# Attention, dense FFN and routed experts on one core: a scratch row 96 bytes longer, the last logits in five per two chunks, two weight splits a chunk earlier

## The chip, the cores and the metric

One core of a Trainium2 chip runs the whole program. Times are device microseconds of one execution; the result of a kernel is the median of several executions. TensorE is PE in the profile (its weight loads PEld), VectorE DVE, ScalarE ACT, GpSimd POOL, and SP issues most of the DMAs.

## The reference, cut to what matters

```python
x = attention(q, k, v)                      # 4 x 8 heads, 576 positions, rotary; -> 2304 tokens x 512
x = square(relu(x @ w_in)) @ w_out          # 512 -> 2048 -> 512
logits = x @ w_gate + modality_bias[modality_id]        # 8 experts
e_idx = argmax(logits, axis=1); gate_w = softmax(logits)[e_idx]
for e in range(8):
    mask = e_idx == e
    out[mask] = gate_w[mask, None] * (relu(x[mask] @ w1[e]) @ w2[e])    # 512 -> 1024 -> 512
```

All of it is float32.

## The kernel before, in words

Attention goes first, by a list of steps written out by hand, and reaches into the start of the dense layer. Then comes `experts`, which this change touches. It works in units, each a pair of matmul groups on TensorE, with two units of lookahead: in unit q the first half of unit q + 2 is issued and then the second half of unit q.

**The dense layer** has 80 units: five blocks of tokens (four of 512, the last of 256) by 16 chunks of 128 hidden features. The first half is `mm1` (12 matmuls: 4 pieces of the contraction by three passes over high and low parts, stationary operand from the weights, moving operand from the tokens `xs`). ScalarE makes `r` and its square `gh`, the low part `gl` comes from VectorE (`rest`, L680), and in the last block ScalarE squares once more into the PSUM tile `h` (L674). The second half is `mm2` (three matmuls for each 128 tokens, stationary `gh` or `gl`, moving the weights, 512 columns).

**The expert layer** has the same shape in units of 128 hidden features of one expert: `emm1` (L984, stationary `w`, moving the gathered tokens `ye` or `yee`), then `emm2` (L1007, stationary `ge`, `geh`, `gel` or `gl`, moving `w`). Each chunk of expert weights is loaded (`eissue`) and split into two parts by ScalarE and VectorE (`esplit`, L937 and L938). Before the first expert its tokens are gathered and transposed (`gtrans`, L957, L970, L971).

**The logits** of a 128-token tile are eight reductions on VectorE (`lg_dve`, L710), whose full-size output `junk` goes to PSUM. Those of the fourth block (three tiles this way, 24 reductions) run in the chunks of the last block, which start at unit n0 = 64; the fourth tile goes over TensorE in the first two chunks (`lg_tr`, `lg_mm`).

**Two resources matter here.** The first is a ring of four PSUM buffers, which `bank` and the tiles `h` take in rotation: each `h`, `tp`, `lp`, `junk` takes the buffer that was taken four requests earlier, and waits until the last reader of that one is done. The second is where tiles lie in SBUF. The weights `wf` and `w`, and the `ye` and `yee` tiles that later take the place of `wf`, are in pools on the left. `we` (the weights of one chunk in sixteen, number 4), `xs`, `r`, and the ring of `gh`, `gl`, `ge`, `geh` and `gel` are in the pool `m_sb` on the right, which ends at the top of the memory. The tiles stand in it in the order of their first use, upwards.

The schedule is a table: `at(mid, n, f)` puts f between the two halves of unit n, `at(pre, n, f)` ahead of both.

Of the kernel before, what the change touches and what calls it, by code (L numbers as in the profile page):

```python
# [9 lines left out]
F32 = mybir.dt.float32  # L10
# [24 lines left out]
def f32(ap):  # L35
    return ap.bitcast(F32)
# [480 lines left out]
def experts(tc, wts, ps, xT, rD, wexp, mod, wg, mb, cst, ident, yD, out):  # L517
    nc = tc.nc
    with ExitStack() as ctx:
        sb = ctx.enter_context(tc.tile_pool(name="m_sb", bufs=1, side="right", reuse_waits="tile"))  # L520
# [12 lines left out]
        def bank(shape, name):  # L533
            return ps.tile(shape, F32, name=name, tag="b", bufs=4)
# [11 lines left out]
        def xraw(b, k):  # L546
            t0, n = BLOCKS[b]
            if b == 1:
                t = wts.pool.tile([128, n], F32, name="xraw", tag="wraw", bufs=NRAW)
                nc.sync.dma_start(out=t, in_=xT[k, :, 0, t0:t0 + n])  # L550
                raws[b, k] = t
                return
            x = t2([128, n], F32, "xraw")
            if k == 0:
                rbs[b] = sb.tile([128, n], F32, name="rbs", tag="xs", bufs=5)
            nc.sync.dma_start(out=x, in_=xT[k, :, 0, t0:t0 + n])
            raws[b, k] = x
            xrec(b, k, rbs[b])
# [16 lines left out]
        def xnorm(b, k, eng):  # L575
            x = raws[b, k]
            eng.tensor_tensor(out=x, in0=x, in1=rbs.pop((b, k)), op=ALU.mult)  # L577

        def xhigh(b, k):
            x = raws[b, k]  # L580
            n, o = BLOCKS[b][1], OFF * (BLOCKS[b][1] <= SLOT)
            t = sb.tile([128, 2 * n + o], F32R, name="xs", tag="xs", bufs=5)
            t = xs[b, k] = t[:, o:o + 2 * n].rearrange("p (a n) -> p a n", a=2)
            nc.scalar.activation(out=t[:, 0], in_=x, func=ACTF.Copy)

        def xlow(b, k):
            t = xs[b, k]
            nc.vector.tensor_tensor(out=t[:, 1], in0=raws.pop((b, k)), in1=f32(t[:, 0]), op=ALU.subtract)
# [119 lines left out]
        def lg_dve(j, e):  # L708
            junk = bank([128, DM], "junk")
            nc.vector.scalar_tensor_tensor(out=junk, in0=ysb[j], scalar=1.0, in1=wgb[e], op0=ALU.mult, op1=ALU.mult,  # L710
                                           accum_out=lg[:, j, e:e + 1])
# [20 lines left out]

        def choose(j0, j1):
            js, shp = slice(j0, j1), [128, j1 - j0, E]
            mx = sb.tile([128, 4], F32, name="mx", tag="mx", bufs=1)[:, 0:j1 - j0]
            km = sb.tile([128, 4], F32, name="km", tag="km", bufs=1)[:, 0:j1 - j0]
            k = sb.tile([128, 4, E], F32, name="ky", tag="ky", bufs=1)[:, 0:j1 - j0]
            d = sb.tile([128, 4, E], F32, name="dl", tag="dl", bufs=1)[:, 0:j1 - j0]
            nc.vector.tensor_tensor(out=lg[:, js], in0=lg[:, js], in1=bias[:, js], op=ALU.add)
            nc.vector.tensor_reduce(out=mx, in_=lg[:, js], axis=AX.X, op=ALU.max)  # L740
            mxb = mx.unsqueeze(2).to_broadcast(shp)
            nc.vector.tensor_tensor(out=k, in0=lg[:, js], in1=mxb, op=ALU.is_ge)
            nc.vector.scalar_tensor_tensor(out=k, in0=k, scalar=-16.0, in1=c_io8.unsqueeze(1).to_broadcast(shp),
                                           op0=ALU.mult, op1=ALU.add)
            nc.vector.tensor_tensor(out=d, in0=lg[:, js], in1=mxb, op=ALU.subtract)
            nc.vector.tensor_reduce(out=km, in_=k, axis=AX.X, op=ALU.min)
            nc.vector.tensor_tensor(out=oh[:, js], in0=k, in1=km.unsqueeze(2).to_broadcast(shp), op=ALU.is_equal)
            nc.vector.tensor_copy(out=ohb[:, js], in_=oh[:, js])
            for j in range(j0, j1):
                nc.vector.tensor_tensor(out=cum[:, j + 1], in0=cum[:, j], in1=ohb[:, j], op=ALU.add)  # L750
            nc.scalar.activation(out=d, in_=d, func=ACTF.Exp)
            nc.vector.tensor_reduce(out=gate[:, js], in_=d, axis=AX.X, op=ALU.add)
            nc.vector.tensor_scalar(out=gate[:, js], in0=gate[:, js], scalar1=1e-9, scalar2=None, op0=ALU.add)
            nc.vector.reciprocal(out=gate[:, js], in_=gate[:, js])

        def ranks(j0, j1):
            js = slice(j0, j1)
            rp = bank([128, j1 - j0, E], "rp")
            nc.tensor.matmul(out=rp, lhsT=lt_b, rhs=ohb[:, js], start=True, stop=False)
            nc.tensor.matmul(out=rp, lhsT=one_b, rhs=cum[:, js], start=False, stop=True)  # L760
            nc.vector.tensor_copy(out=rank[:, js], in_=rp)

        def counts(j):
            cp = bank([128, E], "cp")
            nc.tensor.matmul(out=cp, lhsT=one_b, rhs=cum[:, j], start=True, stop=True)
            tables["n"] = cp
# [158 lines left out]
        def eissue(m):  # L925
            s, f = divmod(m, EFC)
            if f == 0:
                src = es0[0:1, 0:1] if s == NE - 1 else esi[0:1, s:s + 1]
                regs[s] = nc.sync.value_load(src, min_val=0, max_val=E - 1)
            r = wts.pool.tile([128, 1024], F32, name="eraw", tag="wraw", bufs=NRAW)  # L930
            nc.sync.dma_start(out=r, in_=wexp[bass.ds(regs[s], 1), f].rearrange("o p n -> p (o n)"))
            eraw[m] = r

        def esplit(m, nxt=None):
            w = wts.ring.tile([128, 2, 1024], F32R, name="w", tag="w", bufs=NFC - NF0 - NF1)
            r = eraw.pop(m)
            nc.scalar.activation(out=w[:, 0], in_=r, func=ACTF.Copy)  # L937
            nc.vector.tensor_tensor(out=w[:, 1], in0=r, in1=f32(w[:, 0]), op=ALU.subtract)  # L938
            ew[m] = w
            if nxt is not None:  # L940
                eissue(nxt)
# [76 lines left out]
        M0, M1 = (NE - 1) * EFC, (LAST + 1) * EFC  # L1018
        N = NB * NFC
        pre, mid, post = {}, {}, {}  # L1020

        def at(d, n, *fs):
            d.setdefault(n, []).extend(fs)

        at(mid, NFC - 1, load_wgb)
        for b in range(NB):
            if b:
                q = NFC * b
                for k in range(4):
                    if b > 1:  # L1030
                        at(mid, q - 11 + 2 * k, lambda b=b, k=k: xraw(b, k))
                        at(mid, q - 10 + 2 * k, lambda b=b, k=k: xnorm(b, k, nc.gpsimd))
                        at(mid, q - 3, lambda b=b, k=k: [xhigh(b, k), xlow(b, k)])
            j0, nt = BLOCKS[b][0] // 128, BLOCKS[b][1] // 128
            n0 = NFC * (b + 1)
            if b < 3:
                jobs = [(j, e) for j in range(j0, j0 + nt) for e in range(E)]
                for q, (j, e) in enumerate(jobs):
                    at(mid, n0 + q // 3, lambda j=j, e=e: lg_dve(j, e))
                at(mid, n0 + 11, lambda j0=j0, nt=nt: choose(j0, j0 + nt))  # L1040
                if b < 2:
                    at(mid, n0 + 13, lambda j0=j0, nt=nt: ranks(j0, j0 + nt))
                    continue
                at(post, n0 + 13, lambda j0=j0, nt=nt: ranks(j0, j0 + nt), lambda: counts(NT0), early1)
                at(post, n0 + 15, early2)
                at(pre, n0 + 16, early3)
            elif b == 3:
                at(mid, n0, lambda j=j0 + 3: lg_tr(j))
                at(mid, n0 + 1, lambda j=j0 + 3: lg_mm(j))
                for q in range(3 * E):  # L1050
                    at(mid, n0 + q // 2, lambda j=j0 + q % 3, e=q // 3: lg_dve(j, e))
                at(pre, n0 + 8, lambda: [gather(c, True) for c in range(2 * NE)])
                for i in range(4):
                    at(mid, n0 + (3, 6, 9, 12)[i], lambda m=M0 + i: eissue(m))
                    at(pre, n0 + (12, 13, 15, 16)[i], lambda m=M0 + i: esplit(m, m + 4))
                    at(mid, n0 + 10 + i, lambda t=i: gtrans(NE - 1, t))
                at(mid, n0 + 14, lambda j0=j0: choose(j0, j0 + 4))
                at(mid, n0 + 15, lambda j0=j0: ranks(j0, j0 + 4))
# [61 lines left out]
        with tc.If(ns > 2 * LAST + 3):  # L1120
            for s in range(LAST + 1, SLOTS):
# [4 lines left out]
                for f in range(EFC):  # L1126
                    m = s * EFC + f
# [117 lines left out]
```

## Time and profile before

| | us |
|---|---|
| median of 3 executions | 928.31 (927.53 to 929.98) |
| the profiled execution | 926.26 |
| its span in the trace | 924.4 |
| TensorE busy in it | 902.0 (98%) |
| VectorE, ScalarE, GpSimd busy | 634.3, 487.5, 285.4 |

The trace gives each instruction's start and its duration. Matmuls are pipelined: one lasts nearly 400 ns and the next starts some 230 ns after it. What a stretch of matmuls costs is therefore read from the starts, from the first of one group to the first of the next, divided by their number; this text calls it the pitch. Times of the trace count from the span's start.

### The profile page before, as it was taken

To read this page: it belongs to the slowest core of one execution; us is meant where nothing else is said; L and a number is where in the kernel's file an instruction comes from. 1 tells how busy PE (TensorE), PEld (TensorE's weight loads), DVE (VectorE), ACT (ScalarE), POOL (GpSimd) and SP (SyncE) were. 2 spreads that over 40 slices of the span, in tenths; PEclk is the share of its full clock that TensorE was granted. 3 is DMA by queue.
4 is the path that set the end of the run, shared out by engine and by line. 5 is a ranking of instruction groups with operands and counts; after the bars stand their busy time and mean duration, and the time that the engine had idled before them with its cause. 6 is when DMAs were issued, how large, how long until landed. Compare 5 with 4: busy or idle time off the path is not lost. (4 is left out here: it accounts for less than half of the span.)

```text
span 924.4 us, 14539 instructions
## 1 busy us (share of the span) xinstructions
PE 902.0 (98%) x5211; PEld 747.1 (81%) x5211; DVE 634.3 (69%) x1220; ACT 487.5 (53%) x969; POOL 285.4 (31%) x229
## 2 busy tenths in 40 slices
PE   7999999999999999999999999999999999999995
PEld 6778778777877888788788878888988899999994
DVE  7998889999988796665456545655666776666650
ACT  6889799878866663322332232224354265555541
POOL 2667687867445653110010001001000222112111
PEclk9999999999999999999999999999999999999998
DMA  5666645555455445300040002001232567777630
GB/s 172 195 167 198 205 131 189 165 149 171 125 190 174 139 160 146 115 22 1 1 126 12 0 6 87 1 0 57 82 92 69 182 207 263 225 225 236 192 93 36
DMA packets 46976, 115.65 MB, mean 125 GB/s; under 512 B 10272, under 2 KB 14384, under 8 KB 46896
## 3 DMA queue, kind: packets, MB, share of 16 engines
q1 hardware_dynamic: 43856, 104.94, 37.1%
q0 software_dynamic: 3040, 9.70, 3.0%
q8 instruction: 43, 0.70, 0.3%
q14 instruction: 37, 0.30, 0.1%
HBM read 92.56 MB, written 15.54 MB: 117 GB/s over the span
## 5 line engine op out<-in xcount | busy, mean ns | idle before, releaser
L665 ACT ACTIVATE r<-h 128x512 f32<-128x512 f32 (+1 forms) x80 | 44.3, 554 | 222.5 <-PE h L659 202.6
L659 PE MATMUL h<-xs,w 128*128 128x512 f32 (+1 forms) x660 | 147.3, 372 | 0.2 <-DVE gl L680 0.2
L659 PEld LDWEIGHTS h<-xs,w 128*128 128x128 f32 x660 | 116.2, 188 | 25.7 <-DVE gl L680 0.6
L698 PE MATMUL y<-w,gh 128*128 128x512 f32 x396 | 125.2, 397 | 0.0
L285 ACT ACTIVATE e<-sc,nmx 128x576 f32<-128x576 f32 x144 | 106.6, 742 | 33.6 <-DVE nmx L274 32.4
L676 DVE SCALAR_TENSOR_TENSOR h<-h,r 128x512 f32<-128x512 f32 x64 | 44.6, 698 | 116.1 <-ACT r L665 116.1
L274 DVE TENSOR_REDUCE nmx<-sc 128x1 f32<-128x576 f32 x144 | 106.2, 752 | 21.0 <-PE sc L269 17.2
L269 PE MATMUL sc<-kh,q 128*128 128x288 f32 (+1 forms) x336 | 95.6, 322 | 9.3 <-ACT e L285 8.2
L938 DVE TENSOR_TENSOR w<-eraw,w 128x1024 fp32r<-128x1024 f32 x64 | 78.2, 1223 | 32.7 <-ACT w L937 32.7
L269 PE MATMUL sc<-kl,q 128*128 128x288 f32 (+2 forms) x336 | 87.5, 297 | 0.0
L698 PEld LDWEIGHTS y<-w,gh 128*128 128x128 f32 x396 | 73.4, 188 | 16.7
L269 PEld LDWEIGHTS sc<-kh,q 128*128 128x128 f32 x336 | 60.4, 188 | 27.7 <-ACT e L285 20.3
L327 PE MATMUL b<-ident,e 128*128 128x128 f32 x640 | 81.4, 273 | 1.1 <-ACT e L285 1.1
L710 DVE SCALAR_TENSOR_TENSOR junk<-ysb,wgb 128x512 f32<-128x512 f32 x120 | 80.3, 721 | 0.0
L577 POOL TENSOR_TENSOR xraw<-xraw,rbs 128x512 f32<-128x512 f32 (+1 forms) x14 | 16.4, 1177 | 203.0 <-DMA rbs<-rD 174.5
L698 PE MATMUL y<-w,gl 128*128 128x512 f32 x198 | 78.3, 396 | 0.0
L984 PEld LDWEIGHTS h<-ye,w 128*128 128x128 f32 x576 | 74.2, 189 | 4.2
L1007 PE MATMUL y<-w,ge 128*128 128x512 f32 x288 | 75.7, 398 | 0.0
L984 PE MATMUL h<-ye,w 128*128 128x256 f32 x576 | 75.3, 281 | 0.0
L327 PEld LDWEIGHTS b<-ident,e 128*128 128x128 f32 x640 | 73.0, 140 | 1.6 <-ACT e L285 1.3
L356 PE MATMUL b<-et,v 128*64 128x288 f32 x512 | 69.5, 412 | 0.0
L937 ACT ACTIVATE w<-eraw 128x1024 fp32r<-128x1024 f32 x64 | 67.2, 1052 | 4.0 <-DMA eraw<-wexp 4.0
(230 smaller groups left out, 1670.2 us busy)
## 6 DMA issues: line engine op xcount, KB each, us to landing
eraw<-wexp SPq DMA_DIRECT2D x64, 512.0 KB, 4.4
wraw<-wio SPq DMA_DIRECT2D x32, 512.0 KB, 5.1
rawq<-qx SPq DMA_DIRECT2D x15, 576.0 KB, 4.2
rawk<-kx SPq DMA_DIRECT2D x15, 576.0 KB, 4.1
v<-v SPq DMA_DIRECT2D x16, 320.0 KB, 4.7
yD<-ysb SPq DMA_DIRECT2D x18, 256.0 KB, 2.2
xT<-xo SPq DMA_DIRECT2D x12, 288.0 KB, 3.4
xraw<-xT SPq DMA_DIRECT2D x12, 256.0 KB, 2.9
```

Of the source, the lines that this page charges most:

```text
L269: nc.tensor.matmul(out=o[:, x:x + w], lhsT=q[:, hd, q0:q0 + 128], rhs=k[:, hd, y:y + w], start=(n == 0), stop=(n == len(ops) - 1))
L274: nc.vector.tensor_reduce(out=m, in_=sc(p, j)[:, :, 0:HS], axis=AX.XY, op=ALU.max, negate=True)
L285: nc.scalar.activation(out=e(p)[:, o:o + S].rearrange("p (a b) -> p a b", a=2), in_=sc(p, j)[:, :, 0:HS], func=ACTF.Exp, bias=live[p, f"nm ...
L327: nc.tensor.transpose(t[:, i * 128:(i + 1) * 128], x[:, o:o + 128], ident)
L356: nc.tensor.matmul(out=o[64 * hd:64 * hd + 64], lhsT=lhsT, rhs=rhs, start=(c == 0), stop=(c == 4))
L659: nc.tensor.matmul(out=h, lhsT=w[:, a, k * 128:(k + 1) * 128], rhs=xs[b, k][:, c], start=(k == 0 and i == 0), stop=(k == 3 and i == 2))
L698: nc.tensor.matmul(out=yp[t], lhsT=g[a][:, t * 128:(t + 1) * 128], rhs=w[:, c, 512:1024], start=(begin and i == 0), stop=(f == NFC - 1 and ...
L710: nc.vector.scalar_tensor_tensor(out=junk, in0=ysb[j], scalar=1.0, in1=wgb[e], op0=ALU.mult, op1=ALU.mult, accum_out=lg[:, j, e:e + 1])
L937: nc.scalar.activation(out=w[:, 0], in_=r, func=ACTF.Copy)
L938: nc.vector.tensor_tensor(out=w[:, 1], in0=r, in1=f32(w[:, 0]), op=ALU.subtract)
L984: nc.tensor.matmul(out=h, lhsT=w[:, a, k * 128:(k + 1) * 128], rhs=x[:, c], start=(k == 0 and i == 0), stop=(k == 3 and i == 2))
L1007: nc.tensor.matmul(out=yp[s, t], lhsT=g[a][:, t * 128:(t + 1) * 128], rhs=w[:, c, 512:1024], start=(f == 0 and i == 0), stop=(f == EFC - 1 ...
```

## The change

A scratch row `mx` of four numbers is allocated with 28, of which the same four are used. The 24 logit reductions are dealt to the chunks of the last block at five per two chunks (three, two, three, two ...) where there were two per chunk. The loads of three of the first four expert chunks and the splits of the first two are issued one chunk earlier (one load two chunks).

```diff
         def choose(j0, j1):
             js, shp = slice(j0, j1), [128, j1 - j0, E]
-            mx = sb.tile([128, 4], F32, name="mx", tag="mx", bufs=1)[:, 0:j1 - j0]
+            mx = sb.tile([128, 28], F32, name="mx", tag="mx", bufs=1)[:, 0:j1 - j0]
...
                 for q in range(3 * E):
-                    at(mid, n0 + q // 2, lambda j=j0 + q % 3, e=q // 3: lg_dve(j, e))
+                    at(mid, n0 + 2 * q // 5, lambda j=j0 + q % 3, e=q // 3: lg_dve(j, e))
                 at(pre, n0 + 8, lambda: [gather(c, True) for c in range(2 * NE)])
                 for i in range(4):
-                    at(mid, n0 + (3, 6, 9, 12)[i], lambda m=M0 + i: eissue(m))
-                    at(pre, n0 + (12, 13, 15, 16)[i], lambda m=M0 + i: esplit(m, m + 4))
+                    at(mid, n0 + (3, 5, 8, 10)[i], lambda m=M0 + i: eissue(m))
+                    at(pre, n0 + (11, 12, 15, 16)[i], lambda m=M0 + i: esplit(m, m + 4))
                     at(mid, n0 + 10 + i, lambda t=i: gtrans(NE - 1, t))
```

The longer row moves every tile of `m_sb` that stands below it 96 bytes down; nothing outside that pool moves. First bytes in a partition, as the two programs are built:

| tiles | before | after | before modulo 128 | after modulo 128 |
|---|---|---|---|---|
| `wf` (4 buffers, later `yee`) | 41600, 50048, 58496, 66944 | same | 0 | 0 |
| `ye` (in those buffers, 192 bytes in) | 41792, ... | same | 64 | 64 |
| `w` (11 buffers) | 75392 + 8192 i | same | 0 | 0 |
| `we` | 180960 | 180864 | 96 | 0 |
| `xs` of 512 tokens (5 buffers) | 189152 + 4096 i | 189056 + 4096 i | 96 | 0 |
| `xs` of the last block (192 bytes in) | 189344 + 4096 i | 189248 + 4096 i | 32 | 64 |
| `gh`, `gl`, `ge`, `geh`, `gel` (7 buffers) | 213728 + 2048 i | 213632 + 2048 i | 96 | 0 |

Inside these tiles a matmul's operands start at multiples of 512 bytes (1024 in `xs` and `ye` of 256 tokens), so a column of the table holds for every matmul.

On VectorE, in the first chunks of the last block, the order of the two programs differs like this (L710 is a logit, L680 the low part `gl`, L730 the copy of the fourth tile's logits):

```order
-L710 SCALAR_TENSOR_TENSOR junk,lg<-ysb,wgb 128x512 x2
+L710 SCALAR_TENSOR_TENSOR junk,lg<-ysb,wgb 128x512 x3
 L680 TENSOR_TENSOR gl<-h,gh 128x256
 L730 COPY lg<-lp 128x8
```

A third logit, and with it a third request to the PSUM ring, now stands between the `gl` of one chunk and that of the next; this is so in every second chunk, with two in the others.

On VectorE, at the end of the last block, where the gathered tokens are transposed (L971 is the low part of `yee`, L938 the split of expert weights):

```order
 L971 TENSOR_TENSOR yee<-tp,yee 128x2x128 x2
-L680 TENSOR_TENSOR gl<-h,gh 128x256
-L710 SCALAR_TENSOR_TENSOR junk,lg<-ysb,wgb 128x512 x2
+L938 TENSOR_TENSOR w<-eraw,w 128x1024
+L680 TENSOR_TENSOR gl<-h,gh 128x256
 L971 TENSOR_TENSOR yee<-tp,yee 128x2x128 x2
 L938 TENSOR_TENSOR w<-eraw,w 128x1024
 L680 TENSOR_TENSOR gl<-h,gh 128x256
 L971 TENSOR_TENSOR yee<-tp,yee 128x2x128 x2
-L938 TENSOR_TENSOR w<-eraw,w 128x1024
 L680 TENSOR_TENSOR gl<-h,gh 128x256
 L971 TENSOR_TENSOR yee<-tp,yee 128x2x128 x2
```

No logits are left among the four transposes, and the two splits stand ahead of the second and third of them, where they stood ahead of the third and fourth. ScalarE's halves of the splits move with them; the order on SP and POOL is the same in both programs, and so is the order of TensorE's matmuls.

## Rows read from the trace of the kernel before

**Rows 1.** The page: busy time of the engines; the group of the logits.

```profile
PE 902.0 (98%) x5211; PEld 747.1 (81%) x5211; DVE 634.3 (69%) x1220; ACT 487.5 (53%) x969; POOL 285.4 (31%) x229
...
L710 DVE SCALAR_TENSOR_TENSOR junk<-ysb,wgb 128x512 f32<-128x512 f32 x120 | 80.3, 721 | 0.0
```

**Rows 2.** Windows, L698 (`mm2`) alone: stretch, length, PE and PEld busy (count), granted clock, DMA.

```profile
0.00:925.00 925.00, 214.50 (x864) 161.08 (x864) 1.00 0.40 125
```

**Rows 3.** The same for L1007 (`emm2`).

```profile
0.00:925.00 925.00, 117.39 (x456) 82.11 (x456) 1.00 0.40 125
```

**Rows 4.** Groups by form: line, tiles, shapes, count, busy and mean, idle before.

```profile
L659 PE MATMUL h<-xs,w 128*128 128x512 f32 x528 | 130.0, 396 | 0.2 <-DVE gl L680 0.2
...
L984 PE MATMUL h<-ye,w 128*128 128x256 f32 x576 | 75.3, 281 | 0.0
...
L659 PE MATMUL h<-xs,wf 128*128 128x512 f32 x192 | 47.0, 395 | 0.0
```

**Rows 5.** Timeline of TensorE in the fourth block: start, length, instruction, count.

```profile
565.55 2.90 PE L659 MATMUL h<-xs,we 128*128 128x512 f32 x12
568.28 0.63 PE L698 MATMUL y<-wf,gh 128*128 128x512 f32 x2
...
571.08 2.97 PE L659 MATMUL h<-xs,w 128*128 128x512 f32 x12
573.89 0.63 PE L698 MATMUL y<-wf,gh 128*128 128x512 f32 x2
...
579.50 0.62 PE L698 MATMUL y<-we,gh 128*128 128x512 f32 x2
...
582.25 1.09 PE L659 MATMUL h<-xs,w 128*128 128x512 f32 x4
```

**Rows 6.** Timeline of TensorE in the expert layer.

```profile
740.86 4.25 PE L984 MATMUL h<-ye,w 128*128 128x256 f32 x36
744.95 1.55 PE L1007 MATMUL y<-w,ge 128*128 128x512 f32 x6
746.34 1.58 PE L984 MATMUL h<-ye,w 128*128 128x256 f32 x12
747.76 1.55 PE L1007 MATMUL y<-w,ge 128*128 128x512 f32 x6
```

**Rows 7.** Timeline of one chunk of the last block.

```profile
655.27 1.57 PE L659 MATMUL h<-xs,w 128*128 128x256 f32 x12
...
656.67 0.63 PE L698 MATMUL y<-we,gh 128*128 128x512 f32 x2
...
658.01 0.42 DVE L680 TENSOR_TENSOR gl<-h,gh 128x256 fp32r<-128x256 f32 x1 [1.06 <-ACT h L674]
658.07 1.56 PE L659 MATMUL h<-xs,w 128*128 128x256 f32 x12
```

**Rows 8.** Timeline, second chunk of the last block, where the fourth tile is transposed.

```profile
645.89 1.65 PE L659 MATMUL h<-xs,wf 128*128 128x256 f32 x12
645.91 0.69 DVE L720 TENSOR_TENSOR yt<-tp,yt 128x512 fp32r<-128x512 f32 x1
```

**Rows 9.** Timeline, the first two transposes of gathered tokens.

```profile
672.08 1.57 PE L659 MATMUL h<-xs,w 128*128 128x256 f32 x12
...
673.84 0.66 PE L957 MATMUL tp<-ident,gx 128*128 128x128 f32 x4 [0.18 <-DVE junk L710]
...
675.73 1.57 PE L659 MATMUL h<-xs,w 128*128 128x256 f32 x12
...
677.82 0.63 PE L957 MATMUL tp<-ident,gx 128*128 128x128 f32 x4 [0.52 <-PE h L659]
```

**Rows 10.** Timeline, the first matmuls of the expert layer.

```profile
685.96 0.40 PE L698 MATMUL y<-w,gl 128*128 128x512 f32 x1
...
686.50 3.45 PE L984 MATMUL h<-yee,w 128*128 128x512 f32 x12
...
689.79 0.62 PE L698 MATMUL y<-w,gh 128*128 128x512 f32 x2
```

## The prediction

> **What bounds the kernel now.** I read the page first: TensorE is busy for 902.0 us, 98% of the span, and no other engine above 69% [rows 1]; the granted clock is 1.00, its upper level of 2.4 GHz [rows 2]. The reader is to see that from the dense layer on the time is the number of matmuls times their pitch, plus the few places where TensorE waits. A gain has to come out of the pitch or out of those places; whatever ScalarE, VectorE or the DMAs save elsewhere falls into slack. Then I counted the matmuls of 512 columns: 528 + 192 in `mm1` with weights from `w` and `wf` [rows 4], 864 in `mm2` [rows 2], 456 in `emm2` [rows 3]. Then the timeline, for their pitch and for the waits.
>
> The pitch is not the same for equal matmuls. In the fourth block 12 of `mm1` with weights from `we` take 568.28 - 565.55 = 2.73 us, 227.5 ns each; the next 12 of `mm1`, with weights from `w`, take 573.89 - 571.08 = 2.81 us, 234.2 ns each [rows 5]. Between them lie 12 of `mm2`, moving operand from `wf`, at (571.08 - 568.28) / 12 = 233.3 ns; where `mm2` moves `we`, 12 take 582.25 - 579.50 = 2.75 us, 229.2 ns [rows 5]. Shape, passes and the work of the other engines are alike in neighbouring units. What differs is the address. Before the change `we`, `xs`, `gh` and `gl` all start at 96 modulo 128, `w` and `wf` at 0. So a matmul whose moving and stationary operand have the same remainder runs at 227 to 229 ns, and one with unlike remainders at some 234.
>
> **The longer row.** It puts `we`, `xs` and the rings of `gh` and `ge` at remainder 0, where `w` and `wf` are already. From then on every 512-column matmul of both layers has operands with equal remainders. It applies to those that had unlike ones: 528 + 192 = 720 of `mm1`; of the 864 of `mm2` all but the sixteenth part that moves `we`, 864 - 54 = 810; and the 456 of `emm2`, whose moving `w` is at 0 and whose stationary tiles were at 96. That is 1986. The saving of each is open between two ends. Least: `emm2` with unlike remainders takes only (746.34 - 744.95) / 6 = 231.7 ns in a quiet unit [rows 6], and the slower of the equal stretches 229.2: 2.5 ns, 5.0 us in all. Most: from 234.2 to 227.2, twice the 113.6 ns of a 256-column stretch below: 7.0 ns, 13.9 us. I take the mean of the two unlike stretches, 233.7, less 227.5, that is 6.2 ns: the 229.2 begins straight after a stretch with unlike remainders, and after the change there is none left to begin after. 1986 x 6.2 ns = **12.3 us**.
>
> A rule of the Trainium skill speaks against this. "TensorE: Matmul & The Clock Gate", section "Step-by-step: what each phase is for", says that the moving operand and the weight load have read ports of their own and that loading the next weights takes no bandwidth from the running matmul; by it an address could not matter and this term would be 0. The trace does not agree: in rows 5 the same moving tile runs at 227.5 or 234.2 ns with the weights' address. This is the first rival below.
>
> The 256-column matmuls are less clear. `emm1` from `ye` has remainders 64 and 0 before and after, yet it runs at two speeds: 36 in a row at (744.95 - 740.86) / 36 = 113.6 ns, and the usual 12 between two `emm2` at (747.76 - 746.34) / 12 = 118.3 ns [rows 6]. The 36 have no `emm2` among them. I read this as the unlike-remainder `emm2` leaving the stream in a worse step that the following 12 keep; if so, 576 - 36 = 540 of them [rows 4] gain 4.7 ns, 2.5 us, and if the step belongs to the change from one group to the other, nothing. I take half, 1.3 us. The last block's 180 `mm1` with `w` and `wf` (15 of 16 chunks) go from remainders 32 and 0 to 64 and 0; at (656.67 - 655.27) / 12 = 116.7 ns [rows 7] they can gain 0 to 3.1 ns, 0 to 0.6 us; I take 0.3.
>
> **Three logits in a chunk.** In itself a third logit costs nothing: VectorE has room in a chunk of 2.8 us (655.27 to 658.07 [rows 7]), where its `gl` is 0.42 us and a logit 0.72 [rows 1]. It costs through the PSUM ring. With two logits per chunk the requests go h, junk, junk; the buffer four back is a logit's, done long before. With three they go h, junk, junk, junk, h, and the second `h` takes the buffer of the first. That happens at four chunks (the fourth, sixth, eighth and tenth `h` requested in the last block's chunks), and at one more where `lp` stands between and hides it. `mm1` must then wait for the previous chunk's `gl`, which runs from 658.01 to 658.43, while TensorE would start at 658.07 [rows 7]. That is 0.36 us and a hand-over that no row here shows apart; I add 0.09 for it, which makes 0.45 us, four times: 1.8 us. Behind the waiting `mm1` stand the chunk's `mm2` and all later matmuls; ScalarE and VectorE wait for it in turn, so it isn't made good. Once more, in the second chunk, `h` now takes the buffer of the transposed fourth tile, which VectorE reads until 646.60 (645.91 + 0.69); `mm1` starts at 645.89 now [rows 8], so 0.75 us. Together **2.55 us lost**. Its least is 4 x 0.36 + 0.71 = 2.15.
>
> **Logits out of the way, splits earlier.** The first transpose waits for a logit's buffer: 12 matmuls from 672.08 at 116.7 ns end at 673.48, the transpose starts at 673.84, 0.36 us; the second at 677.82 instead of 677.13, 0.69 us [rows 9]. With the logits finished by the tenth chunk the buffers that they take are two chunks old, and both waits go. The first `emm1` starts at 686.50 where 685.96 + 0.23 would do, and its 12 take 689.79 - 686.50 = 3.29 us instead of 12 x 0.228 = 2.74 [rows 10]; 0.85 us in all, since ScalarE does a weight split before the last transposed tile. Without that split most of it goes; I leave 0.15, because the low part still comes after the high part. Gain 0.36 + 0.69 + 0.70 = **1.75 us**. The splits' new places cost nothing: TensorE is what they run beside, and what reads them comes chunks later. On SP the loads stand in the same order as before, so no queue is passed.
>
> **Sum.** 12.3 + 1.3 + 0.3 + 1.75 - 2.55 = 13.1 us. The profiled execution took 926.26 us, so 913.2; it lies 2.05 us under the median of the runs shown, so the median to expect is **915.2 us**.
>
> **The rivals.** (1) Addresses do nothing; what `we` shows is something about its chunk. Then only the schedule is left: 2.55 - 1.75 = 0.8 us more, 929.1 us. For it: the rule above. Against it: the same chunk's weights are fast as stationary operand in `mm1` and as moving one in `mm2`, at different times beside different work [rows 5]. (2) Equal remainders help, but the stream falls out of step at each change of group, and the 256-column ones keep theirs: 2.5 to 4 ns on 1986, less 0.8: 4 to 7 us, so 921 to 924 us. For it: the 229.2 [rows 5]. (3) Slower: the address does nothing and the third logit doesn't fit. If three logits pushed back the next `gl`, each of the five chunks with three would lose a further logit of 0.72 us [rows 1], 3.6 us in all: 926.26 + 0.8 + 3.6 + 2.05 = 932.7 us. It decides once VectorE's `gl` and three logits exceed the chunk; 0.42 + 3 x 0.72 = 2.6 against 2.8 us [rows 1, 7] speaks against it, though narrowly. (4) A faster TensorE finds VectorE late: at 69% over the whole span [rows 1] it has room for the 1.4% that I ask for; this would only cut the gain, as (2).
>
> **How the numbers follow.** Full effect 0.75, partial (2) and (4) 0.13, none 0.08, slower 0.04. About 0.3%, 2.8 us, is what a measurement of this kernel can tell from no change. Everything at its best, 13.9 + 2.5 + 0.6 + 1.75 = 18.8 us, gives 909.5; the partial case reaches to 924. The range is 909.5 to 923, which leaves out rivals (1) and (3) and the edge of (2), under 2 in 10. Faster 0.88, same 0.08, slower 0.04.
>
> **What would show it.** Right: `mm1` with `w` no slower than with `we`, both at 227 to 228 ns; `emm2` too; the last chunks' transposes without a wait, and `mm1` of four chunks of the last block waiting some 0.45 us for `gl`. Wrong: a pitch of 234 ns where both remainders are 0. The prediction fails if the pitch depends on the distance of the two addresses in another way than by the remainder, for `w` and `xs` lie elsewhere than `we` and `xs`.

## The result, and the profile after

The changed kernel takes 918.63 us (median of four runs, 917.37 to 919.39); the kernel before, beside it on the same chip, 927.92 us (926.67 to 929.98, four runs). The ratio is 0.9896, 95% interval 0.9874 to 0.9918: faster by some 1%, inside the range forecast and 3.4 us above the predicted time. Timed a second time (below), the ratio was 0.9921 (0.9903 to 0.9939), a gain of 7.4 us.

The page of after, against [rows 1]: TensorE does the same 5211 instructions in 10 us less.

```profile
PE 891.7 (97%) x5211; PEld 747.2 (81%) x5211; DVE 635.9 (69%) x1220; ACT 487.0 (53%) x969; POOL 286.5 (31%) x229
```

The timeline of TensorE of after in the fourth block, for [rows 5] (start, length, instruction, count):

```profile
562.18 2.88 PE L659 MATMUL h<-xs,we 128*128 128x512 f32 x12
564.90 0.62 PE L698 MATMUL y<-wf,gh 128*128 128x512 f32 x2
...
567.62 2.88 PE L659 MATMUL h<-xs,w 128*128 128x512 f32 x12
570.34 0.62 PE L698 MATMUL y<-wf,gh 128*128 128x512 f32 x2
...
573.06 2.88 PE L659 MATMUL h<-xs,w 128*128 128x512 f32 x12
```

From start to start every group of twelve now takes 2.72 us, 226.7 ns a matmul: `mm1` with `we`, `mm1` with `w` (234.2 before) and the `mm2` between them (233.3 before). That is the forecast sign, at the fast edge of the forecast 227 to 228.

The expert layer of after, same columns, for [rows 6]:

```profile
798.10 1.64 PE L1007 MATMUL y<-w,ge 128*128 128x512 f32 x6
799.57 1.53 PE L984 MATMUL h<-ye,w 128*128 128x256 f32 x12
800.94 1.54 PE L1007 MATMUL y<-w,ge 128*128 128x512 f32 x6
802.32 1.58 PE L984 MATMUL h<-ye,w 128*128 128x256 f32 x12
803.73 1.52 PE L1007 MATMUL y<-w,ge 128*128 128x512 f32 x6
805.09 1.58 PE L984 MATMUL h<-ye,w 128*128 128x256 f32 x12
```

Two steps are seen here. Behind a disturbed group, six `emm2` take 1.38 us (230.0 ns) and twelve `emm1` 1.37 us (114.2 ns); once the stream has settled, `emm2` takes (805.09 - 803.73) / 6 = 226.7 ns, and `emm1` (803.73 - 802.32) / 12 = 117.5 ns. In this kernel `emm1` does not gain with `emm2`, as I had assumed; its fast step goes with the slow one of `emm2`.

The last block of after, TensorE and VectorE, at two of the five places where a third logit shifts the PSUM ring ([rows 7, 8]):

```profile
640.30 0.40 PE L698 MATMUL y<-wf,gl 128*128 128x512 f32 x1
640.56 0.69 DVE L720 TENSOR_TENSOR yt<-tp,yt 128x512 fp32r<-128x512 f32 x1
641.30 1.67 PE L659 MATMUL h<-xs,wf 128*128 128x256 f32 x12 [0.61 <-DVE yt L720]
...
647.63 0.39 PE L698 MATMUL y<-wf,gl 128*128 128x512 f32 x1
647.84 0.42 DVE L680 TENSOR_TENSOR gl<-h,gh 128x256 fp32r<-128x256 f32 x1 [1.68 <-ACT h L674]
648.32 1.65 PE L659 MATMUL h<-xs,w 128*128 128x256 f32 x12 [0.30 <-DVE gl L680]
649.81 0.63 PE L698 MATMUL y<-wf,gh 128*128 128x512 f32 x2
```

`gl` ends at 648.26; `mm1`, which could have started at 647.63 + 0.23 = 647.86, starts at 648.32, and its twelve take 1.49 us instead of 1.41: 0.46 + 0.08, the second part in the first two matmuls (222 ns apart instead of 118). The same wait stands at 653.74, 659.84 and 665.92, and the one for `yt` at 640.30 costs 0.78 + 0.11: 4 x 0.54 + 0.89 = 3.05, some 3.1 us against a stream that never waits. The 0.11 is hardly new: these twelve last 1.67 us now and lasted 1.65 us before [rows 8], so against the kernel before the loss is some 3.0 us.

The transposes and the first matmuls of the expert layer, for [rows 9, 10]:

```profile
669.49 1.58 PE L659 MATMUL h<-xs,w 128*128 128x256 f32 x12
670.90 0.60 PE L957 MATMUL tp<-ident,gx 128*128 128x128 f32 x4
...
672.72 1.53 PE L659 MATMUL h<-xs,w 128*128 128x256 f32 x12
674.10 0.60 PE L957 MATMUL tp<-ident,gx 128*128 128x128 f32 x4
...
682.33 3.15 PE L984 MATMUL h<-yee,w 128*128 128x512 f32 x12
685.32 0.62 PE L698 MATMUL y<-w,gh 128*128 128x512 f32 x2
```

The first two transposes follow their twelve matmuls after 1.41 and 1.38 us, without a wait, and the first `emm1` take 2.99 us, not 3.29.

One wait was not forecast. In the first block TensorE now stands for GpSimd's low part of a weight half-chunk (the row of GpSimd is L514):

```profile
358.84 2.55 POOL L577 TENSOR_TENSOR xraw<-xraw,rbs 128x512 f32<-128x512 f32 x2 [2.78 <-DMA xraw<-xT]
361.35 1.72 POOL L514 TENSOR_TENSOR w<-wmag,w 128x512 fp32r<-128x512 f32 x1
...
361.62 0.39 PE L698 MATMUL y<-w,gh 128*128 128x512 f32 x1
363.12 0.50 PE L698 MATMUL y<-w,gh 128*128 128x512 f32 x1 [1.11 <-POOL w L514]
```

The same low part in the kernel before, and the pair of matmuls of which the second needs it:

```profile
358.97 1.29 POOL L514 TENSOR_TENSOR w<-wmag,w 128x512 fp32r<-128x512 f32 x1
360.43 0.63 PE L698 MATMUL y<-w,gh 128*128 128x512 f32 x2
```

There the low part was done at 360.26 and the matmul due at 360.43 + 0.23 = 360.66: the split was done 0.4 us before TensorE came. Counted from each kernel's first `mm1` (279.10 and 281.79) the split ends at 81.2 and 81.3 us, while TensorE is there after 81.6 us before and 80.1 us after. A stage in which TensorE had no wait had hardly any slack either.

**The ledger.** The starts of the matmuls, followed from the first `mm1` to the last matmul, span 635.4 us before and 625.9 after, 9.5 us less. The distances from start to start, waits left out, add up by group to: `mm1` and other L659 matmuls of 512 columns 179.05, then 174.17; `mm2` and `emm2` 307.28, then 299.99; `emm1` of 256 columns 67.80, then 67.34; `mm1` of 256 columns 22.53, then 22.37. The waits at the ring cost 3.0 more than before, those at transposes and first `emm1` give back some 1.6, and waits on operands elsewhere cost 2.2 in after (first block 0.37 + 0.19 + 1.28, routing 0.36) against 0.33 before. -12.8 + 3.0 - 1.6 + 1.9 = -9.5. The profiled pair itself differs by only 926.26 - 919.39 = 6.9 us, because attention, whose code is the same, ended 2.7 us later in the profiled run of after (281.79 against 279.10).

### The profile page after: what moved, and what is told of

Same layout as the page of the kernel before. It is cut to its first block, busy times and chain, and to the rows that moved or that the text cites. A ratio compares the mean times of both kernels' runs of the same rounds, so it can differ in the third digit from the quotient of the medians.

```text
span 917.6 us, 14540 instructions
## 1 busy us (share of the span) xinstructions
PE 891.7 (97%) x5211; PEld 747.2 (81%) x5211; DVE 635.9 (69%) x1220; ACT 487.0 (53%) x969; POOL 286.5 (31%) x229
## 5 line engine op out<-in xcount | busy, mean ns | idle before, releaser
L659 PE MATMUL h<-xs,w 128*128 128x512 f32 (+1 forms) x660 | 143.9, 368 | 1.2 <-DVE gl L680 1.2
L659 PEld LDWEIGHTS h<-xs,w 128*128 128x128 f32 x660 | 115.7, 188 | 24.0 <-DVE gl L680 2.9
L698 PE MATMUL y<-w,gh 128*128 128x512 f32 x396 | 123.2, 391 | 1.1 <-POOL w L514 1.1
L938 DVE TENSOR_TENSOR w<-eraw,w 128x1024 fp32r<-128x1024 f32 x64 | 78.3, 1225 | 32.4 <-ACT w L937 32.2
L698 PEld LDWEIGHTS y<-w,gh 128*128 128x128 f32 x396 | 73.3, 188 | 16.4 <-POOL w L514 1.5
L710 DVE SCALAR_TENSOR_TENSOR junk<-ysb,wgb 128x512 f32<-128x512 f32 x120 | 81.1, 729 | 0.0
L698 PE MATMUL y<-w,gl 128*128 128x512 f32 x198 | 77.2, 390 | 0.2 <-DVE gl L680 0.2
L1007 PE MATMUL y<-w,ge 128*128 128x512 f32 x288 | 74.6, 394 | 0.0
```

The costliest lines, as they stand in the source:

```text
L659: nc.tensor.matmul(out=h, lhsT=w[:, a, k * 128:(k + 1) * 128], rhs=xs[b, k][:, c], start=(k == 0 and i == 0), stop=(k == 3 and i == 2))
L698: nc.tensor.matmul(out=yp[t], lhsT=g[a][:, t * 128:(t + 1) * 128], rhs=w[:, c, 512:1024], start=(begin and i == 0), stop=(f == NFC - 1 and ...
L1007: nc.tensor.matmul(out=yp[s, t], lhsT=g[a][:, t * 128:(t + 1) * 128], rhs=w[:, c, 512:1024], start=(f == 0 and i == 0), stop=(f == EFC - 1 ...
```

## The experiments

Lines shift by a few where an edit adds some; the pitches below are means over all matmuls of the group, from start to start, with waits left out.

**The longer row alone** (`e1_row_only`; schedule as before).

```
-            mx = sb.tile([128, 4], F32, name="mx", tag="mx", bufs=1)[:, 0:j1 - j0]
+            mx = sb.tile([128, 28], F32, name="mx", tag="mx", bufs=1)[:, 0:j1 - j0]
```

> Only the row is longer; logits and splits stand as before. Theory (the pitch goes by the remainders of the two operands' addresses modulo 128): nearly all of the gain is here, and since the changed kernel shows four waits of 0.56 us and one of 0.89 us for the PSUM ring and only 1.7 us given back at the first transposes, this kernel is about 1 us faster than the changed one: 916.5 to 918 us, 512-column pitch 227 ns. It must still show the waits of the first two transposes (0.36 and 0.69 us). Rival (the gain comes from the logits and splits): no faster than before, 928 us.

Measured 919.18 us against 928.53 before, ratio 0.9893 (0.9873 to 0.9913). All 512-column groups run at 226.8 to 228.4 ns. The waits at the transposes are there as before, those at the ring are not, and the one for the low part of L514 is. From the view of TensorE's waits (what waits and for what: us in total, times, longest):

```profile
PE y L698 <- POOL w L514: 1.3, 1, 1.3
PE tp L957 <- PE h L659: 0.5, 1, 0.5
```

So the gain is the row's, and it is also what makes the split late. The expected lead of about 1 us over the changed kernel did not show: 919.18 us is above the 916.5 to 918 expected, and from the first `mm1` to the last matmul it takes 625.5 us against the changed kernel's 625.9. The schedule's part is small against the row's.

**The schedule alone** (`e2_schedule_only`; row of 16 bytes): the other three changed lines of the diff.

> Only the logits and the splits are moved; the row is as before. Theory: the sum of 3.1 us lost at the ring and 1.7 us given back is left, 1 to 1.5 us slower than before, 929 us, pitch 232 to 238 ns as before, and none of the waits of TensorE for a product of GpSimd in the first block that the changed kernel shows, since TensorE comes no earlier there. Rival (the schedule brings the gain): 919 us.

Measured 929.52 us, ratio 1.0011 (0.9997 to 1.0024); pitches as before (`mm1` with `w` 233.8). The same view shows the ring and nothing at L514:

```profile
PE h L659 <- DVE gl L680: 1.0, 4, 0.3
PE h L659 <- DVE yt L720: 0.6, 1, 0.6
```

By itself the schedule costs about as much as the 0.8 us forecast (636.3 us from the first `mm1` to the last matmul, against 635.4 before); the interval of the times doesn't exclude nothing.

**Other remainders** (`e3_remainder_64`, `e4_remainder_96_again`, `e7_remainder_32`): rows of 12, 36 and 20 floats, schedule as before.

```
-            mx = sb.tile([128, 4], F32, ...
+            mx = sb.tile([128, 12], F32, ...     (36 and 20 in the other two)
```

> The row has 12 numbers, so the right pool moves by 32 bytes and its large tiles start at 64 modulo 128, those of the left pool at 0; schedule as before. If equality modulo 128 counts: pitch of mm1 with w, of mm2 and of emm2 233 ns, time as before, 928 us, and only mm1 and mm2 with we at 227 ns. If equality modulo 64 is enough: 227 ns everywhere, 916.5 to 918 us. Rival (any move helps, for instance because a tile no longer shares something with another): also fast.

> The row has 36 numbers, so the right pool moves by 128 bytes, further than in the changed kernel, and its tiles start at 96 modulo 128 again; schedule as before. Theory: pitch as before (227 ns with we, 231 to 238 ns with w), 928 us. Rival (what helps is that the tiles lie lower, not the remainder): 227 ns and 917 us.

> A row of 80 bytes: `we`, `xs` and the ring at remainder 32 modulo 128, `w` and `wf` at 0; schedule as before. Theory of equality modulo 128: `mm1` with `w`, `mm2` and `emm2` stay at 232 to 234 ns, with `we` (32 and 32) 227 to 229; the time is that of the kernel before, 926 to 929 us. Rival, that some unequal remainders are as good as equal ones: 227 ns in all, some 916 to 919 us.

Remainder 64 gave 926.24 us, ratio 0.9983 (0.9968 to 0.9997): `mm1` with `w` 231.5 ns, `mm2` with `w` 233.3; it is thus a little faster than before, which none of its expectations had. Remainder 96 again, 128 bytes further, gave 927.82 us in one run, `mm1` with `w` 233.3 ns; remainder 32 gave 929.77 us in one run, 233.2 ns. In all three, `mm1` with `we` runs at 227 to 230 ns. So it isn't that the buffers lie lower, nor that the row is longer, and equality modulo 64 is not enough: of four remainders only the weights' own brings 227 ns. With remainder 32 the expert layer does something of its own:

```profile
795.74 1.55 PE L1007 MATMUL y<-w,ge 128*128 128x512 f32 x6
797.13 1.54 PE L984 MATMUL h<-ye,w 128*128 128x256 f32 x12
798.50 1.56 PE L1007 MATMUL y<-w,ge 128*128 128x512 f32 x6
799.90 1.54 PE L984 MATMUL h<-ye,w 128*128 128x256 f32 x12
```

`emm1` takes (798.50 - 797.13) / 12 = 114.2 ns, `emm2` (799.90 - 798.50) / 6 = 233.3. A unit of eighteen takes 799.90 - 797.13 = 2.77 us, just as in after (805.09 - 802.32 = 2.77) and less than the 747.76 - 746.34 + 1.39 = 2.81 of before [rows 6]. So this unit gains as much over before while its `emm2` stays slow: `emm1` gains in its place. No unit shown here has both at their fastest.

**`we` and `xs` alone** (`e5_xs_alone`): 96 bytes of padding between the tiles, so that the ring of `gh` and `ge` keeps its address.

```
+            small([128, 24], F32, "pad")
```

> The row of 16 bytes and the schedule stay as before; 96 bytes are put below the tiles of the expert layers' right pool that hold `we` and `xs` but above `r` and the ring of `gh` and `ge`, so that only `we` and `xs` come to remainder 0 modulo 128 and the ring stays at 96. Theory that each matmul needs its own two operands at equal remainders: the 720 512-column `mm1` with `w` and `wf` fall from 233.8 to some 227 ns, `mm2` with `w` and `wf` stays at 233.5, the 54 `mm2` that move `we` rise from 229 to some 233.5, `emm2` stays at some 232; 720 x 6.2 - 54 x 4.5 = 4.2 us, so some 924 us. Rival, that the pitch goes with where the pool as a whole lies, or with the ring of `gh` and `ge` alone: `mm1` stays at 233.8 and the time at 928, or all groups fall to 227 and the time is 916.

Measured 925.98 us against 928.60, ratio 0.9968 (0.9953 to 0.9984): 2.6 us less where 4.2 was expected, which the interval (1.5 to 4.4 us) just includes; from the first `mm1` to the last matmul it is 631.8 us against 635.4. Its timeline in the fourth block:

```profile
573.04 2.89 PE L659 MATMUL h<-xs,w 128*128 128x512 f32 x12
575.77 0.62 PE L699 MATMUL y<-wf,gh 128*128 128x512 f32 x2
...
578.58 2.89 PE L659 MATMUL h<-xs,w 128*128 128x512 f32 x12
581.31 0.62 PE L699 MATMUL y<-we,gh 128*128 128x512 f32 x2
...
584.12 2.89 PE L659 MATMUL h<-xs,w 128*128 128x512 f32 x12
```

`mm1` with `w` falls to 2.73 / 12 = 227.5 ns; `mm2` with `wf` stays at 2.81 / 12 = 234.2; and `mm2` with `we`, 229.2 before, rises to 234.2, because `we` has now left the ring's remainder. This is the cleanest of the runs: within one kernel, neighbouring groups are fast or slow by their own two operands, and one that was fast is made slow.

**`ye` at other remainders** (`e6_ye_remainder_0`, `e11_ye_remainder_32`): the changed kernel with another offset in the row of `ye` and of the last block's `xs`.

```
-OFF = 48
+OFF = 32                     (40 in e11)
```

> The changed kernel, with the offset of `ye` and of the last block's `xs` in their rows 128 bytes instead of 192, so that they lie at remainder 0 like the weights. Theory that equal remainders are what counts for 256 columns too: the 576 `emm1` fall from 116.8 to some 113.6 ns and the last block's 180 `mm1` likewise, (576 + 180) x 3.2 = 2.4 us, some 916 us. Rival, that the 256-column matmuls have their pitch from something else (a gap at each change of group or of weights): both stay within 0.5 ns and the time is that of the changed kernel, 918.6 us.

> The changed kernel with the offset of `ye` and of the last block's `xs` 160 bytes instead of 192, so that they lie at remainder 32 while weights and rings are at 0. Seen so far: `emm1` at 116.8 ns with 64, at 119.6 ns with 0, and the `emm2` behind slower with 0. If the 256-column pitch goes with the distance of `ye` from the weights, 32 lies between: some 118 ns, 919 to 921 us. If it is the remainder 64 alone that is good, as with 0: 120 ns, 921 to 922 us. If unlike remainders of any other size are as good as 64: 117 ns and 918.6 us.

Measured 921.78 us, ratio 0.9933 (0.9907 to 0.9960), with remainder 0; and with 32, 920.88 us, ratio 0.9922 (0.9897 to 0.9947), which can't be told from the changed kernel's 920.42 on the same chip. Neither theory for remainder 0 held. Its `emm1` rose to 119.6 ns, and the `emm2` between them to some 233, with both of their own operands at 0:

```profile
802.21 1.55 PE L1007 MATMUL y<-w,ge 128*128 128x512 f32 x6
803.61 1.60 PE L984 MATMUL h<-ye,w 128*128 128x256 f32 x12
805.04 1.56 PE L1007 MATMUL y<-w,ge 128*128 128x512 f32 x6
806.45 1.60 PE L984 MATMUL h<-ye,w 128*128 128x256 f32 x12
```

A unit takes 806.45 - 803.61 = 2.84 us against 2.77. With 32, `emm1` takes 118.7 ns, as the first of its expectations had it (by the distance from the weights), and `emm2` some 230. So a matmul's own two remainders don't decide alone: what the 256-column matmuls around it leave behind does too.

Not all that these two profiled runs take longer is pitch. In both the granted clock stood at its lower level of 1.2 GHz for a stretch behind the routing, and twelve `emm1` from `yee` took 4.56 us, where they take 3.00 in after: 1.56 us. First remainder 0 (timeline, then the stretch with its length, TensorE busy and count, granted clock, DMA share, GB/s), then after:

```profile
722.31 4.56 PE L984 MATMUL h<-yee,w 128*128 128x512 f32 x12
723.00:726.00 3.00, 3.00 (x8) 0.50 0.55 169
```

```profile
724.01 3.00 PE L984 MATMUL h<-yee,w 128*128 128x512 f32 x12
```

TensorE did the same before it in all three: a wait of 0.2 us and eighteen short matmuls.

The run with remainder 0 also bears on the modulus. `w` and `wf` start at 128 modulo 256 (75392, 41600 ...), and so do all tiles whose 512-column matmuls run at 227 ns in after; there, equal modulo 128 is always equal modulo 256 too. `ye` at remainder 0 starts at 41600 + 128 = 41728, which is 0 modulo 256: of all pairs named here only those with it and with the last block's `xs` of that run are equal modulo 128 and not modulo 256, and `emm1` is slow there. With distances of 64, 96 and 128 bytes modulo 256 between `ye` and the weights, `emm1` takes 116.9, 118.7 and 119.6 ns. This speaks for 256 and doesn't show it, since these are 256-column matmuls; a row `mx` of 60 numbers, which would put `xs` and the rings at 0 modulo 256, was not tried.

**The ring** (`e8_changed_again`, `e9_one_logit_buffer`), the changed kernel once more and with one buffer for the logits of a chunk:

```
+        def sink(n):
+            if n not in sinks:
+                sinks[n] = bank([128, DM], "junk")
+            return sinks[n]
...
-            junk = bank([128, DM], "junk")
+            junk = bank([128, DM], "junk") if n is None else sink(n)
```

> The changed kernel unaltered, timed beside the next two kernels on one chip so that they can be set against it: 918.6 us, a ratio to the kernel before of 0.9895.

> The changed kernel with one PSUM buffer for all logits of a chunk in the last block instead of one each, so that the ring's requests go h, junk, h, junk as before the change had h, junk, junk. Theory that the third logit costs only through the ring: the four waits of `mm1` for the previous chunk's `gl` go (4 x 0.56 = 2.2 us), and the one for `yt` too unless the transposed tile still lies four requests back (0.89 us); 2.2 to 3.1 us under the changed kernel, 915.5 to 916.4 us. Rival, that the waits would come back elsewhere, because the logits still hold VectorE when the next `gl` is due: TensorE waits for `gl` or `gh` as long as before, 918.6 us.

Measured 920.42 us (ratio 0.9921, 0.9903 to 0.9939; 1.8 us above the expected) and 916.41 us (0.9885, 0.9859 to 0.9910), beside 927.79 before. The five waits at the ring are gone; at the chunk shown above `mm1` starts as soon as `mm2` is through:

```profile
647.28 0.39 PE L698 MATMUL y<-wf,gl 128*128 128x512 f32 x1
647.51 1.58 PE L659 MATMUL h<-xs,w 128*128 128x256 f32 x12
648.92 0.62 PE L698 MATMUL y<-wf,gh 128*128 128x512 f32 x2
```

The third logit costs through the ring and in no other way: VectorE has room for it. The medians differ by 4.0 us where the waits removed add up to 3.1; runs of one kernel scatter by more than the rest.

**The late split** (`e10_low_part_on_vector`): the one-buffer kernel with one word of the written order changed.

```
-16.wl25.P
+16.wl25.V
```

> As the one-buffer kernel, and one weight split, the low part of half-chunk 25, is done by VectorE instead of GpSimd, where in the changed kernel it starts behind two `xraw` operations at 361.35 us and TensorE waits for it in the first block. Theory that the faster pitch of the first block has made this split late: the wait of 1.1 us at 361.62 us goes, 0.7 to 1.1 us under the one-buffer kernel, some 915 us. Rival, that VectorE is the late one in the first block: TensorE waits there for `gl` or for the next low part instead, and the time is that of the one-buffer kernel.

Measured 914.26 us, ratio 0.9863 (0.9840 to 0.9885), the fastest of all. TensorE's waits of this kernel from the first block on:

```profile
PE h L659 <- DVE gl L680: 0.3, 1, 0.3
PE y L698 <- DVE gl L680: 0.2, 1, 0.2
PE mp L797 <- DVE ohr L788: 0.2, 1, 0.2
```

The wait for L514 is gone and none took its place in that block (the 0.2 us for `gl` was there in after; the 0.3 us, at 390.35, is in the second block, where the kernel before waits 0.2). From the first `mm1` to the last matmul it takes 622.4 us, against 626.6 in the run of the changed kernel beside it; the expected 3.1 + 1.1 is the same 4.2.

## Why the prediction was right, and where it was off

**The longer row.** The mechanism held, in its sign and its size. 1986 matmuls at 6.2 ns were to give 12.3 us; the 512-column groups of the ledger give (179.05 - 174.17) + (307.28 - 299.99) = 12.2. The experiment with `we` and `xs` alone shows that in the dense layer the pair of operands decides, and those with remainders 32, 64 and 96 that unlike ones cost; whether the modulus is 128, as the prediction has it, or 256 stays open. Rival (1) falls: the pitch moved with addresses alone, from 234.2 to 226.7 ns. By the rule of the Trainium skill that the prediction set against itself ("TensorE: Matmul & The Clock Gate", section "Step-by-step: what each phase is for"), loading weights takes no bandwidth from the running matmul. The prediction took from it that this term would be 0, and the trace doesn't agree with that.

**The 256-column matmuls** failed as a reading. I forecast 1.3 + 0.3 us, on the view that unlike-remainder `emm2` leave the stream in a worse step and equal ones would cure it. They gained 0.46 + 0.16 us. The step does depend on what goes before, but not in that way: in after 117.5 ns goes with `emm2` at 226.7, and 114.2 with `emm2` at 230. Nor is the opposite a rule, for the kernel before has 118.3 beside 231.7 [rows 6], and with `ye` at remainder 0 it is 119.6 beside 233. The 36 in a row at 113.6 ns before [rows 6] were one such state of the stream, no sign of what settled groups would reach.

**Three logits in a chunk.** The five places, their cause and their order were right. The term was mis-sized: some 3.0 us against 2.55. The start of `mm1` came late by 0.46 where I had 0.45, but I left out that the first two matmuls after such a wait lie 0.1 us further apart; the wait for `yt` came to 0.78 where I had 0.75.

**Logits out of the way.** 1.75 us was forecast, some 1.6 measured: both waits of the transposes gone, the wait ahead of the first `emm1` gone, and its twelve shorter by 0.3.

**Rival (4)** came true in a small way: a faster TensorE found its supply late, 1.9 us net. Most of it, 1.28 us, is GpSimd's split; the rest is VectorE's (`gl` 0.37, a split 0.19, the routing 0.36, less the 0.33 that the kernel before has too). I had looked for it in VectorE's 69% [rows 1], a mean over the whole span; what mattered was one split in the first block that ended only 0.4 us before its matmul was due.

Forecast 13.1 us, measured 9.5 on the part of the program that the change touches. Of the 3.6 us between, 1.1 are the 256-column and 512-column pitches together (13.9 against 12.8), 0.45 the ring, 0.15 the give-back and 1.9 the late operands, 3.6 in all. The medians, 918.63 and 927.92, differ by 9.3, so they say the same; those of the second timing differ by 7.4. Every term that missed did so on the same side, so no error made another good.

**Open.** Why the remainder modulo 128 of the two operands matters, and why `ye` at remainder 0 makes both itself and the `emm2` behind it slower, no run shows, and neither is the modulus settled between 128 and 256.

## What to carry to other kernels

When TensorE bounds a kernel, compare the start-to-start pitch of equal matmuls that differ only in their tiles; 3% of that pitch lay here in the addresses of large tiles, which the length of a small scratch tile in the same pool shifts, so it is worth fixing large tiles' addresses on purpose. Before a speed-up of the bounding engine, look not for waits that exist but for operands that arrive just in time, and count the buffers of a shared ring again whenever an extra request is put into an interval. A logit whose product is thrown away needs no buffer of its own.

## What the hardware showed that was not expected

Matmuls of 512 columns ran at 227 to 230 ns with moving and stationary tile at equal remainders modulo 128 bytes (in all these pairs modulo 256 too), and at 231.5 to 234 ns at remainders that differ by 32, 64 or 96; `emm2` between `emm1` with `ye` at remainder 0 took 233 in spite of equal ones. Matmuls of 256 columns had two steps, about 114 and 118 ns, which the stream falls into with what goes before, and 120 ns with `ye` at remainder 0.

The attention stage, with the same code in all kernels, ended between 278.8 and 284.1 us in the profiled runs. Part of it is the granted clock early on. The stretch from 15 to 40 us, first in a run of before, then in that with `we` and `xs` alone (stretch, length, TensorE busy and count, granted clock, DMA share, GB/s):

```profile
15.00:40.00 25.00, 21.05 (x145) 1.00 0.53 172
```

```profile
15.00:40.00 25.00, 21.15 (x117) 0.80 0.46 146
```

Under 0.80, a mean of stretches at 2.4 and at 1.2 GHz, 28 fewer matmuls were done. TensorE was busy for about as long in both, so this row doesn't say why the clock fell. Differences of 2 or 3 us between single runs of this kernel mean nothing; the distances between matmuls behind the first `mm1` do.
